# A fused convolution and maxout kernel: a reordered opening, a gate made a transfer, sums in three parts, one logarithm one group later, and a last copy split over two engines

## The chip, the cores and the metric

The kernel runs on one core of a Trainium2 chip. The metric is the device time of one execution in microseconds (us). Five engines work in order, each on its own list of instructions: PE (TensorE, matrix products), DVE (VectorE), ACT (ScalarE), POOL (GpSimd) and SP (SyncE, which here only issues transfers). An instruction waits on semaphores for what it needs, and everything behind it on its engine waits with it.

## What is computed

A dynamic convolution over the sequence is followed by a feed-forward layer with a maximum in it. Cut to what matters:

```
w = softmax(weight_gen, over the 7 taps)          # [8, 4160, 8 heads, 7]
y[s] = sum over k of w[s, k] * x[s - 6 + k]       # per head, 24 features each, D = 192
g = maximum(y @ w1, y @ w2)                       # 33280 tokens, 1024 hidden features
out = g @ w_out                                   # [33280, 192], float32
```

## The kernel before

**The tokens.** 33280 tokens lie as 128 partitions by 260 columns. Columns go in 17 batches of 16 (the last has 8), batches in units of 8 columns (of 4 in the first two batches and at the end). A tile of the hidden layer is 1024 values by 128 partitions; there are 260 tiles, in 90 groups, the first eight of two tiles and the others of three (the last of one).

**The softmax** is done as exp(w - ln(sum(exp(w)))): ACT takes the exponential (`exp_sum`, line 153), DVE the sums over taps (`red`, line 168), ACT the logarithm (`ln`, line 172), DVE the subtraction (`shift`, line 177) and ACT the final exponential into `en_t` (`weights`, line 191).

**The convolution.** DVE multiplies x by the weights for all 7 taps into `m_t` (`mul`, line 211). In the first two batches PE adds the taps, one unit at a time, while it transposes (`sum_transpose`, line 281), and ACT copies the result out of the accumulator (`sums_out`, line 293). From batch 2 on DVE adds the taps in three instructions (`adds`, lines 227, 233 and 236), a DMA transposes `y_t` into `yt` (line 245), and the work for later batches is put between the three additions by the `beside` callback: sums in two halves, subtractions in three parts.

**The feed-forward.** max(a, b) is written as a + relu(b - a). PE makes the hidden tiles (`hid_tile`, line 336) from `yt` and `wd` = w2 - w1, ACT applies relu (line 346), PE adds the product with w1 @ w_out (line 388) and the hidden part (line 376), ACT copies the result to `o_t` (line 434) and SP stores it. Half of the hidden part (`out_second`) starts only behind a `relay`, an empty instruction on ACT that waits for the other half.

**The gate.** After each transposing DMA, line 253 has POOL copy one column of `yt` into a small tile `gate`. POOL works in order, so the loads of x and of the weights behind it (lines 125 and 118) are issued only once the transposed unit is there.

**The opening.** Until the steady loop begins (group 8), the order of all work is a list of steps written out by hand, `OPENING`. A step is put on the list of its engine in that order. `lg lw lt xf` are loads issued by SP, `lx lo lh` loads issued by POOL (`@step` holds a load until that step is done). On ACT: `X` exponential, `l` logarithm, `W` weights, `c` casts of w1, `e` copy of a summed unit, `T` copies of turned weights, `r` relu, `V` copies of w1 transposed, `C` copies of w1 @ w_out, `xa` a cast of x, `B` the relay, `E` the copy of the results. On DVE: `n` sums, `s` subtraction, `m` products, `d` the difference w2 - w1, `xv` a cast of x. On PE: `k` products that only keep the clock up, `y` tap sums, `t` turned weights, `h` hidden tiles, `v` and `p` the w1 products, `A` and `D` the two halves of the result. So `W.0.12` is the weights of batch 0 from column 12, `r.3` is the relu of tile 3, and `m.0.0.1` is the second half of the products of the first unit.

The accumulators of `y` (all but the first half unit), `t.0`, `t.1`, `v`, `p` and `A` take turns in two buffers (tag `op`): each waits until the one two before it has been read out. `t.2` shares the buffer of `t.0`. The buffers of `h` take turns in two others.

**The loop** places the ACT softmax steps by a table `SOFTMAX_AT`, keyed by group and place: place 0 is ahead of the last relu of a group, place 1 after its result copy.

Of the kernel before, what the change touches and what calls it, by code (L numbers as in the profile page):

```python
# [9 lines left out]
FP32 = mybir.dt.float32  # L10
BF16 = mybir.dt.bfloat16
# [12 lines left out]
def kernel(  # L24
# [9 lines left out]
    nc = tc.nc  # L34
# [182 lines left out]
    def adds(b, o, first=False, beside=lambda i, of: None):  # L217


        w = dict(pieces(b))[o]  # L220
        n = w * D

        def taps(at, step, cnt):
            return _sub(m_t, K * o * D + at * n, [[step * n, cnt], [1, w * D]])

        beside(0, 3)
        nc.vector.tensor_tensor(out=taps(0, 1, 3), in0=taps(0, 1, 3), in1=taps(3, 1, 3), op=ALU.add)  # L227
        if first:
            return
        beside(1, 3)  # L230
        if b not in y_ts:
            y_ts[b] = py.tile([P, 16 * D], BF16, name="y_t", tag="y")
        nc.vector.tensor_tensor(out=taps(0, 2, 2), in0=taps(0, 2, 2), in1=taps(1, 5, 2), op=ALU.add)  # L233
        beside(2, 3)

        nc.vector.tensor_tensor(  # L236
            out=_sub(y_ts[b], o * D, [[64, 2], [P, 3 * w // 2], [1, 64]]),
            in0=taps(0, 1, 1), in1=taps(2, 1, 1), op=ALU.add,
        )

    def transpose(u):

        b, o, n = UNITS[u]
        yt = pyt.tile([P, 8 // 2 * 3 * P], BF16, name="yt", tag="yt")
        nc.sync.dma_start_transpose(
            out=yt[:, 0:n // 2 * 3 * P].rearrange("p (b t) -> p b t", t=P),
            in_=y_ts[b][:, o * D:(o + n) * D],
        )
        yt_ts[u] = yt
        while held:  # L250
            held.pop(0)()

        nc.gpsimd.tensor_copy(out=gate, in_=yt[:, 0:1])  # L253
# [11 lines left out]
        return slice(64 * j, 64 * j + 64)  # L265


    LEFT = (0, 1, 2, K - 1)

    def sum_transpose(u, i=None):  # L270

        b, o, n = UNITS[u]
        assert n == 4
        to = "h" if i == 0 else "o"
        yps = yps_of[u, i] = ps[to].tile([P, 1024], FP32, name="yps", tag="hd" if i == 0 else "op")
        ks = range(6) if i is None else range(3 * i, 3 * i + 3)
        for k in ks:
            for t in range(K):
                at = K * o * D + (t * 6 + k if i is None else (K * i + t) * 3 + k % 3) * P
                for r in range(2):  # L280
                    nc.tensor.matmul(  # L281
                        yps[:, r * 512 + k * 64:r * 512 + (k + 1) * 64],
                        lhsT=m_t[half(r), at:at + P], rhs=ident[half(r), half(r)],
                        start=(k == ks[0] and t == 0), stop=(t == K - 1),
                        skip_group_check=True,
                    )
# [129 lines left out]
    def evac(p, n):  # L416

        tile_, at = op_at[p]
        o = o_t[0]
        if p == NT // 2 - 1:  # L420

            nc.scalar.copy(out=_sub(o_last, 0, [[D, 2], [1, D]]),
                           in_=_sub(tile_, at, [[512, 2], [1, D]]))
            for j, eng in enumerate((nc.scalar, nc.sync)):
                eng.dma_start(
                    out=bass.AP(tensor=out.tensor, offset=dcol(place(p)[0] + 2 * j) * D, ap=[[CPP * D, P], [1, D]]),
                    in_=o_last[:, j * D:(j + 1) * D],
                )
            return
        runs = [[q for q in range(p, p + n) if column(2 * q)[0] == u]  # L430
                for u in range(column(2 * p)[0], column(2 * (p + n - 1))[0] + 1)]
        for qs in runs:
            c, h = place(qs[0])
            copied = nc.scalar.copy(out=_sub(o, c % 24 * D, [[D, len(qs)], [h * D, 2], [1, D]]),  # L434
                           in_=_sub(tile_, at + (qs[0] - p) * D, [[D, len(qs)], [512, 2], [1, D]]))
        stores = []
        for q in range(p, p + n):
            u, i, _ = column(2 * q)
            if u == NU - 2 and UNITS[u][2] == 8 and i % 2:
                stores.append((nc.sync, place(q)[0] - 1, [4 * D, 2], [1, 2 * D]))  # L440
            elif u < NU - 1 and i == UNITS[u][2] // 2 - 1:
                w = i + 1
                for k in range(0, 2 * w, w if u in PARTED else 2 * w):
                    stores.append((nc.sync, place(q)[0] - i + k, [1, (w if u in PARTED else 2 * w) * D]))
            if u == NU - 1:
                stores.append((nc.sync, place(q)[0], [2 * D, 2], [1, D]))
        for eng, c, *ap in stores:

            def issue(eng=eng, c=c, ap=ap, o=o):
                eng.dma_start(  # L450
                    out=bass.AP(tensor=out.tensor, offset=dcol(c) * D, ap=[[CPP * D, P], *ap]),
                    in_=_sub(o, c % 24 * D, ap),
                )

            if 3 <= u < NU - 3:
                held.append(issue)
            else:
                while u > 3 and held:
                    held.pop(0)()
                issue()  # L460
        return copied
# [80 lines left out]
    around = consts.tile([P, 2 * P], BF16, name="around")  # L542
    ident, swap = around[:, 0:P], around[:, 64:64 + P]
    zeros = consts.tile([P, PAD * D], BF16, name="zeros")
    gate = consts.tile([P, 1], FP32, name="gate")
    o_last = consts.tile([P, 2 * D], FP32, name="o_last")

    pstage = ctx.enter_context(ExitStack())
    stage = pstage.enter_context(tc.tile_pool(name="pstage", bufs=1))
# [13 lines left out]
    def load_w(h, wi):  # L563

        wsrc = (moe_w1, moe_w2)[wi]
        return nc.sync.dma_start(
            out=ws["E", wi][:, h * HF:(h + 1) * HF],
            in_=bass.AP(tensor=wsrc.tensor, offset=h * HF, ap=[[F, P], [1, HF]]),
        )

    def load_last(h, wi):

        wsrc = (moe_w1, moe_w2)[wi]
        return nc.sync.dma_start(  # L574
            out=ws["T", wi][half(h), :],
            in_=bass.AP(tensor=wsrc.tensor, offset=P * F + h * HF, ap=[[F, 64], [1, HF]]),
        )
# [124 lines left out]
    def results_buffer(_):  # L702
# [16 lines left out]
    }  # L719

    OPENING = """
        lg.0 xf.-6.6 xf.0.4 lt.1.0 lt.0.0 k.2 lw.0.1 k.19 lw.0.0 lt.1.1 lw.1.0 lt.0.1 X.0.0.2 k.1 n.0.0.2
        X.0.1.2 lw.1.1 k.1 k.2 n.0.1.2 l.0.0.2 s.0.0.2 xa.-6.4 l.0.1.2 W.0.0.0 lx.0.4.4@l.0.0.2 lg.1 xv.-2.6
        W.0.0.1 s.0.1.2 W.0.12 c.0 lx.0.12.4@W.0.12 W.0.8 m.0.0.0 m.0.0.1 W.0.4 y.0.0 y.0.1 c.2 e.0.0 c.1
        e.0.1 d.0 d.2 t.0 k.3 t.2 T.3 d.1 T.4 h.0 h.1 t.1 X.1 r.0 lx.0.8.4 T.1 lo.0 r.1 m.0.4 n.1 v.0 h.2
        lx.1.0.8 V.1 y.1 r.2 l.1 h.3 e.1 m.0.8 lg.2@l.1 s.1 V.0 m.0.12 r.3 h.4 W.1.0 m.1.0 y.2 h.5 r.4 p.0
        e.2 r.5 h.6 lx.1.8.8@r.4 lg.3@e.2 y.3 W.1.8 h.7 lh.2 C.1 C.0 C.2 A.3 W.1.4 X.2 r.6 e.3 B.3 m.1.4 h.8
        D.3 y.4 r.7 r.8 Z.0 E.3 n.2 X.3 l.2 m.1.8 A.4 e.4 W.1.12 lx.2.0.8.0@r.7 B.4 h.9 D.4 h.10 r.9 E.4 s.2
        r.10 lg.4@r.9 y.5 W.2.0 A.5 h.11 B.5 h.12 e.5 D.5 n.3 r.11 r.12 A.6 m.1.12 E.5 h.13 B.6 D.6 y.6 r.13
        E.6 h.14 e.6 l.3 lx.2.8.8@r.13 h.15 r.14 A.7 W.2.8 B.7 y.7 D.7 r.15 e.7 E.7  # L730
    """

    make_identity(nc, ident_f)
# [3 lines left out]
    for step in OPENING.split():  # L737
# [24 lines left out]
    def extra(t):  # L762

        u, k = TILES[t]
        b, o, n = UNITS[u]
        s = o + k

        if s == 0 and b + 1 < NB:
            mul(b + 1, 0)
        later = 0 if b < 4 else 5  # L770
        if s == later and b + 1 < NB:

            c = b + 1
            adds(c, 0, beside=lambda i, of: shift(c + 1, i, of) if c + 1 < NB else None)
        if s == 8 and b + 2 < NB:
            mul(b + 1, 8)
        if s == 8 + later and b + 2 < NB:
            adds(b + 1, 8, beside=lambda i, of: red(b + 3, i, 2) if b + 3 < NB and i < 2 else None)
        if s == 8 and b + 2 == NB:
            mul(b + 1, 4)  # L780
            adds(b + 1, 4)
        if k == n // 4 - 1 and 7 < u + 1 < NU:
            transpose(u + 1)
# [41 lines left out]
```

## Time and profile before

| what | value |
|---|---|
| median of 3 runs | 405.51 us (405.4 to 405.52) |
| the profiled execution | 405.37 us, with a span of 403.6 us |
| PE busy | 394.8 us, 98% of the span |
| DVE busy | 369.1 us, 91%, done at 376.3 us |
| ACT busy | 360.9 us, 89% |
| POOL busy | 72.3 us, of which the 30 gate copies 39.9 us |
| granted TensorE clock | 1.00 throughout |

The span is from the first instruction's start to the last one's end; 1.8 us of the profiled execution's time lie outside it. An engine's busy share over the whole span hides that the opening, the loop and the tail have different limits: PE is idle or on clock-keeping products for much of the first 30 us, and without a gap from then until the last product.

### The profile page before, as it was taken

Reading aid. Unit: us, or ns where it says so; the run is one execution under the profiler, and the core shown is the slowest. Engines: PE = TensorE matmul, PEld = TensorE weight load, DVE = VectorE, ACT = ScalarE, POOL = GpSimd, SP = SyncE. Lnnn points to the kernel's source line nnn. Section 1 sums busy time; section 2 is a strip of 40 time slices with the busy share of each in tenths; the row PEclk is TensorE's granted clock in tenths of the full one; section 3 lists DMA queues with packets and bytes.
Section 4 is the critical chain, followed back from the end, with each engine's and each line's share of the span. In section 5 each row is a group of like instructions: output and inputs, shape, how many; then the busy total and the mean of one; then the engine's idle time right before and its main releaser. Section 6 shows DMA issues by size and latency. Waiting matters only on the chain.

```text
span 403.6 us, 16321 instructions
## 1 busy us (share of the span) xinstructions
PE 394.8 (98%) x7499; PEld 321.3 (80%) x7499; DVE 369.1 (91%) x211; ACT 360.9 (89%) x466; POOL 72.3 (18%) x96
## 2 busy tenths in 40 slices
PE   7799999999999999999999999999999999999996
PEld 3589999777778777778777778877777877787996
DVE  5999999999999999999999999999999999998200
ACT  5999899999999989999899999989999899888872
POOL 3111031211122210222220122122012121200000
PEclk9999999999999999999999999999999999999999
DMA  8956468767768646864766667777457847558304
GB/s 262 222 140 151 120 124 167 183 164 133 190 110 222 182 79 129 240 187 80 217 187 107 141 192 193 99 215 198 81 115 228 178 80 200 141 106 193 104 31 169
DMA packets 60883, 63.16 MB, mean 157 GB/s; under 512 B 47641, under 2 KB 48665, under 8 KB 60816
## 3 DMA queue, kind: packets, MB, share of 16 engines
q1 hardware_dynamic: 52816, 40.15, 36.4%
q0 software_dynamic: 7856, 21.89, 27.4%
q8 instruction: 58, 0.95, 1.0%
q10 hardware_dynamic: 144, 0.10, 0.1%
q14 instruction: 9, 0.07, 0.1%
HBM read 36.55 MB, written 25.56 MB: 154 GB/s over the span
## 4 chain that ended last, share of the span: by engine, by line
PE 92%; ACT 5%; DMA 1%; SPq 1%; issue 0%
PE op_ps L376 42%; PE hdc L336 13%; PE hdb L336 13%; PE hda L336 13%; PE op_ps L388 8%; ACT rd_t L346 2%; DMA ws0E<-in_moe_w_dram 1%; PE hdp L336 1%; PE yps L281 1%; ACT en_t L191 1%; ACT yt L293 1%; ACT e_t L153 0%; ACT w1t L644 0%; SPq L574 0%; ACT w L622 0%
## 5 line engine op out<-in xcount | busy, mean ns | idle before, releaser
L376 PE MATMUL op_ps<-wo,rd_t 64*128 64x192 bf16 x4160 | 210.6, 243 | 0.0
L376 PEld LDWEIGHTS <-rd_t 64*128 64x128 bf16 x4160 | 181.0, 94 | 14.7
L211 DVE TENSOR_TENSOR m_t<-xb,en_t 128x10752 bf16<-128x10752 bf16 (+2 forms) x39 | 187.8, 4821 | 1.5 <-ACT en_t L191 1.4
L336 PEld LDWEIGHTS <-wd 64*128 64x128 bf16 x1824 | 96.8, 94 | 40.4 <-issue 2.5
L346 ACT ACTIVATE rd_t<-hdc 128x1024 bf16<-128x1024 f32 x82 | 84.1, 1025 | 17.8 <-PE hdc L336 16.2
L253 POOL CAST gate<-yt 128x1 f32<-128x1 bf16 x30 | 39.9, 1332 | 271.3 <-DMA yt<-y_t 271.3
L346 ACT ACTIVATE rd_t<-hda 128x1024 bf16<-128x1024 f32 x81 | 83.4, 1030 | 0.2 <-ACT o_t L434 0.2
L346 ACT ACTIVATE rd_t<-hdb 128x1024 bf16<-128x1024 f32 x81 | 83.5, 1031 | 0.0
L227 DVE TENSOR_TENSOR m_t<-m_t 128x4608 bf16<-128x4608 bf16 (+1 forms) x30 | 73.0, 2433 | 0.1
L336 PE MATMUL hdc<-yt,wd 64*128 64x512 bf16 (+1 forms) x552 | 67.9, 353 | 0.0
L434 ACT COPY o_t<-op_ps 128x384 f32<-128x384 f32 (+1 forms) x99 | 56.1, 577 | 12.4 <-PE op_ps L376 12.3
L336 PE MATMUL hdb<-yt,wd 64*128 64x512 bf16 (+1 forms) x540 | 67.1, 355 | 0.0
L336 PE MATMUL hda<-yt,wd 64*128 64x512 bf16 (+1 forms) x540 | 67.1, 355 | 0.0
L388 PE MATMUL op_ps<-w,yt 64*128 64x192 bf16 x780 | 55.5, 243 | 0.0
L388 PEld LDWEIGHTS <-yt 64*128 64x128 bf16 x780 | 39.0, 94 | 14.5 <-issue 0.3
L233 DVE TENSOR_TENSOR m_t<-m_t 128x3072 bf16<-128x3072 bf16 (+1 forms) x30 | 50.2, 1674 | 0.1
L191 ACT ACTIVATE en_t<-wg_t 128x896 bf16<-128x896 f32 (+3 forms) x48 | 35.7, 773 | 3.0 <-PE op_ps L376 2.0
L236 DVE TENSOR_TENSOR y_t<-m_t 128x1536 bf16<-128x1536 bf16 (+1 forms) x30 | 27.5, 916 | 0.6
L177 DVE TENSOR_TENSOR wg_t<-wg_t,sum_t 128x280 f32<-128x280 f32 (+6 forms) x46 | 22.2, 483 | 0.0
L168 DVE TENSOR_REDUCE sum_t<-e_t 128x64 f32<-128x448 f32 (+3 forms) x31 | 19.7, 639 | 2.3 <-ACT e_t L153 2.3
L125 POOL DMA_DIRECT2D xb<-in_x_dram x34 | 18.2, 537 | 17.3 <-ACT rd_t L346 11.0
L153 ACT ACTIVATE e_t<-wg_t 128x896 f32<-128x896 f32 (+2 forms) x18 | 15.9, 886 | 2.1 <-DMA wg_t<-in_weight_gen_dram 2.1
(40 smaller groups left out, 110.0 us busy)
## 6 DMA issues: line engine op xcount, KB each, us to landing
out_dram<-o_t SPq DMA_DIRECT2D x21, 768.0 KB, 4.3
xb<-in_x_dram POOLq DMA_DIRECT2D x30, 384.0 KB, 5.0
out_dram<-o_t SPq DMA_DIRECT2D x22, 384.0 KB, 3.7
wg_t<-in_weight_gen_dram POOLq DMA_DIRECT2D x13, 448.0 KB, 5.7
xb<-xb POOLq DMA_DIRECT2D x7, 288.0 KB, 5.1
wg_t<-in_weight_gen_dram SPq DMA_DIRECT2D x2, 448.0 KB, 5.2
xb<-in_x_dram POOLq DMA_DIRECT2D x4, 192.0 KB, 6.4
xs<-in_x_dram SPq DMA_DIRECT2D x1, 576.0 KB, 4.3
```

Of the source, the lines that this page charges most:

```text
L177: nc.vector.tensor_tensor(out=w_t, in0=w_t, in1=_sub(s_ts[b], hs.start, [[1, hs.stop - hs.start], [0, K]]), op=ALU.subtract)
L191: act = nc.scalar.activation(out=_sub(en_ts[b], (o * WGC + ((i or 0) * J + j) * N * K) * 2, [[2 * N, K], [2, N], [1, 2]]), in_=_sub(wg_ts[ ...
L211: return nc.vector.tensor_tensor(out=m_out, in0=x_in, in1=_sub(en_ts[b], at * H * 2, [[2, K * n * H], [0, G // 2], [1, 2]]), op=ALU.mult,)
L227: nc.vector.tensor_tensor(out=taps(0, 1, 3), in0=taps(0, 1, 3), in1=taps(3, 1, 3), op=ALU.add)
L233: nc.vector.tensor_tensor(out=taps(0, 2, 2), in0=taps(0, 2, 2), in1=taps(1, 5, 2), op=ALU.add)
L236: nc.vector.tensor_tensor(out=_sub(y_ts[b], o * D, [[64, 2], [P, 3 * w // 2], [1, 64]]), in0=taps(0, 1, 1), in1=taps(2, 1, 1), op=ALU.add,)
L253: nc.gpsimd.tensor_copy(out=gate, in_=yt[:, 0:1])
L336: nc.tensor.matmul(hid_out(t, f, j), lhsT=wd_at(j, s, f // 4, f % 4 * P, P), rhs=_sub(yt_ts[u][half(j), :], (s + j) % 3 * P, [[3 * P, w // ...
L346: relu_of[t0] = nc.scalar.activation(out=rd[:, k * 1024:(k + n) * 1024], in_=hd[:, at:at + n * 1024], func=AF.Relu)
L376: return nc.tensor.matmul(op_out(c), lhsT=rd[rows, k * 1024 + at:k * 1024 + at + P], rhs=wo[rows, f * D:(f + 1) * D], start=False, stop=(r ...
L388: nc.tensor.matmul(op_out(c + j), lhsT=yt_ts[u][half(j), (3 * i + (s + j) % 3) * P:(3 * i + (s + j) % 3 + 1) * P], rhs=w10[half(j), s * D: ...
L434: copied = nc.scalar.copy(out=_sub(o, c % 24 * D, [[D, len(qs)], [h * D, 2], [1, D]]), in_=_sub(tile_, at + (qs[0] - p) * D, [[D, len(qs)] ...
```

## The change

Five edits. In `OPENING` the steps stand in another order, and several loads are held by other steps. The gate becomes a transfer of two values issued by POOL. The sums of the loop are taken in three parts, one ahead of each of the three additions. The logarithm of batch 5 moves from group 16 to group 17. The last result is copied in two halves, one by ACT and one by DVE, into two tiles.

```diff
-        nc.gpsimd.tensor_copy(out=gate, in_=yt[:, 0:1])
+        nc.gpsimd.dma_start(out=gate, in_=yt[0:1, 0:2])
...
-            nc.scalar.copy(out=_sub(o_last, 0, [[D, 2], [1, D]]),
-                           in_=_sub(tile_, at, [[512, 2], [1, D]]))
-            for j, eng in enumerate((nc.scalar, nc.sync)):
+            for j, (eng, copy) in enumerate(((nc.scalar, nc.scalar.copy), (nc.sync, nc.vector.tensor_copy))):
+                copy(out=o_last[j], in_=tile_[:, at + 512 * j:at + 512 * j + D])
...
-        lg.0 xf.-6.6 xf.0.4 lt.1.0 lt.0.0 k.2 lw.0.1 k.19 lw.0.0 lt.1.1 lw.1.0 lt.0.1 X.0.0.2 k.1 n.0.0.2
-        X.0.1.2 lw.1.1 k.1 k.2 n.0.1.2 l.0.0.2 s.0.0.2 xa.-6.4 l.0.1.2 W.0.0.0 lx.0.4.4@l.0.0.2 lg.1 xv.-2.6
-        W.0.0.1 s.0.1.2 W.0.12 c.0 lx.0.12.4@W.0.12 W.0.8 m.0.0.0 m.0.0.1 W.0.4 y.0.0 y.0.1 c.2 e.0.0 c.1
-        e.0.1 d.0 d.2 t.0 k.3 t.2 T.3 d.1 T.4 h.0 h.1 t.1 X.1 r.0 lx.0.8.4 T.1 lo.0 r.1 m.0.4 n.1 v.0 h.2
-        lx.1.0.8 V.1 y.1 r.2 l.1 h.3 e.1 m.0.8 lg.2@l.1 s.1 V.0 m.0.12 r.3 h.4 W.1.0 m.1.0 y.2 h.5 r.4 p.0
-        e.2 r.5 h.6 lx.1.8.8@r.4 lg.3@e.2 y.3 W.1.8 h.7 lh.2 C.1 C.0 C.2 A.3 W.1.4 X.2 r.6 e.3 B.3 m.1.4 h.8
-        D.3 y.4 r.7 r.8 Z.0 E.3 n.2 X.3 l.2 m.1.8 A.4 e.4 W.1.12 lx.2.0.8.0@r.7 B.4 h.9 D.4 h.10 r.9 E.4 s.2
-        r.10 lg.4@r.9 y.5 W.2.0 A.5 h.11 B.5 h.12 e.5 D.5 n.3 r.11 r.12 A.6 m.1.12 E.5 h.13 B.6 D.6 y.6 r.13
-        E.6 h.14 e.6 l.3 lx.2.8.8@r.13 h.15 r.14 A.7 W.2.8 B.7 y.7 D.7 r.15 e.7 E.7
+        lg.0 k.2 xf.-6.6 xf.0.4 lt.1.0 lt.0.0 lw.0.1 lw.0.0 lt.1.1 lw.1.0 lt.0.1 X.0.0.2 n.0.0.2 X.0.1.2
+        lw.1.1 n.0.1.2 l.0.0.2 k.19 s.0.0.2 l.0.1.2 xa.-6.4 W.0.0.0 xv.-2.6 lx.0.4.4@xa.-6.4 lg.1 s.0.1.2
+        W.0.0.1 k.1 lx.0.12.4@W.0.0.1 c.0 m.0.0.0 c.2 d.0 m.0.0.1 y.0.0 t.0 k.3 W.0.4 e.0.0 W.0.12 k.2 y.0.1
+        d.2 W.0.8 e.0.1 t.2 d.1 T.4 T.3 t.1 T.1 h.0 k.1 h.1 c.1 lx.0.8.4@e.0.0 lg.2@e.0.1 lo.0 r.0 X.1 h.2
+        r.1 m.0.4 v.0 n.1 V.0 lx.1.0.8@r.1 y.1 r.2 l.1 h.3 e.1 m.0.8 r.3 V.1 s.1 m.0.12 h.4 W.1.0 y.2 r.4
+        W.1.8 m.1.0 h.5 p.0 e.2 h.6 C.2 C.1 y.3 lx.1.8.8@C.2 r.5 lg.3@W.1.0 lh.2 h.7 C.0 A.3 X.2 r.6 W.1.4
+        n.2 h.8 l.2 B.3 e.3 D.3 r.7 y.4 Z.0 E.3 A.4 m.1.4 X.3 W.1.12 h.9 B.4 r.8 e.4 m.1.8 r.9 D.4 s.2 lg.4
+        h.10 E.4 n.3 lx.2.0.8.0@r.8 r.10 y.5 h.11 W.2.0 A.5 B.5 h.12 e.5 D.5 r.11 A.6 l.3 h.13 E.5 r.12 B.6
+        W.2.8 D.6 h.14 E.6 m.1.12 y.6 r.13 e.6 h.15 A.7 lx.2.8.8@W.2.8 r.14 B.7 y.7 D.7 r.15 e.7 E.7
...
-        (9, 1): "X.4 W.3.0", (12, 0): "W.3.8 l.4", (14, 1): "X.5", (16, 0): "W.4.0", (16, 1): "l.5",
+        (9, 1): "X.4 W.3.0", (12, 0): "W.3.8 l.4", (14, 1): "X.5", (16, 0): "W.4.0", (17, 1): "l.5",
...
-            adds(b + 1, 8, beside=lambda i, of: red(b + 3, i, 2) if b + 3 < NB and i < 2 else None)
+            adds(b + 1, 8, beside=lambda i, of: red(b + 3, i, 3) if b + 3 < NB else None)
```

The diff also lets `sum_transpose` leave out taps of units in a set `fewer`, lets `load_w` load a whole matrix and `load_last` use another queue. No step uses these: the set stays empty, so PE has the same instructions in number and kind.

More of the change, by code (lines that the diff above doesn't have):

```diff
@@ L228, in adds @@
         if first:
+            fewer.add((b, o))
             return
@@ L265, in half @@
         return slice(64 * j, 64 * j + 64)
-    LEFT = (0, 1, 2, K - 1)
+    fewer = set()
     def sum_transpose(u, i=None):
@@ L276, in sum_transpose @@
         ks = range(6) if i is None else range(3 * i, 3 * i + 3)
+        taps = (0, 1, 2, K - 1) if (b, o) in fewer else range(K)
         for k in ks:
-            for t in range(K):
+            for t in taps:
                 at = K * o * D + (t * 6 + k if i is None else (K * i + t) * 3 + k % 3) * P
@@ L420, in evac @@
         if p == NT // 2 - 1:
-            nc.scalar.copy(out=_sub(o_last, 0, [[D, 2], [1, D]]),
-                           in_=_sub(tile_, at, [[512, 2], [1, D]]))
-            for j, eng in enumerate((nc.scalar, nc.sync)):
+            for j, (eng, copy) in enumerate(((nc.scalar, nc.scalar.copy), (nc.sync, nc.vector.tensor_copy))):
+                copy(out=o_last[j], in_=tile_[:, at + 512 * j:at + 512 * j + D])
                 eng.dma_start(
                     out=bass.AP(tensor=out.tensor, offset=dcol(place(p)[0] + 2 * j) * D, ap=[[CPP * D, P], [1, D]]),
-                    in_=o_last[:, j * D:(j + 1) * D],
+                    in_=o_last[j],
                 )
@@ L544 @@
     zeros = consts.tile([P, PAD * D], BF16, name="zeros")
-    gate = consts.tile([P, 1], FP32, name="gate")
-    o_last = consts.tile([P, 2 * D], FP32, name="o_last")
+    gate = consts.tile([1, 2], BF16, name="gate")
+    o_last = [consts.tile([P, D], FP32, name=f"o_last{j}") for j in range(2)]
     pstage = ctx.enter_context(ExitStack())
@@ L565, in load_w, with load_last @@
         wsrc = (moe_w1, moe_w2)[wi]
+        at, w = (0, F) if h == 2 else (h * HF, HF)
         return nc.sync.dma_start(
-            out=ws["E", wi][:, h * HF:(h + 1) * HF],
-            in_=bass.AP(tensor=wsrc.tensor, offset=h * HF, ap=[[F, P], [1, HF]]),
+            out=ws["E", wi][:, at:at + w],
+            in_=bass.AP(tensor=wsrc.tensor, offset=at, ap=[[F, P], [1, w]]),
         )
-    def load_last(h, wi):
+    def load_last(h, wi, act=0):
         wsrc = (moe_w1, moe_w2)[wi]
-        return nc.sync.dma_start(
+        return (nc.scalar if act else nc.sync).dma_start(
             out=ws["T", wi][half(h), :],
```

## The prediction

> **What bounds the kernel now.** I read the page's busy digits first, then PE's waits.
>
> ```profile
> PE   7799999999999999999999999999999999999996
> DVE  5999999999999999999999999999999999998200
> PE hdp L336 <- ACT yt L293: 1.3, 2, 0.8
> PE hdp L336 <- ACT rd_t L346: 0.4, 1, 0.4
> ```
>
> PE loses time in the first quarters only. The windows of the trace give it 10.0 of 10.0 us busy from 30 to 40 us, and every later window up to 395 us full as well; its last wait is that of h.8 on r.6, ending at 29.36 us. So the end is set by when PE gets through the opening, as long as the other engines keep ahead. In the opening the one without gaps is ACT, by its own timeline from 8 to 31 us:
>
> ```profile
> 9.95 0.62 ACT L622 CAST w<-ws0E 128x512 bf16<-128x512 f32 x1 [1.02 <-DMA ws0E<-in_moe_w_dram]
> 10.48 1.29 ACT L191 ACTIVATE en_t<-wg_t 128x224 bf16<-128x224 f32 x4
> ...
> 13.45 1.08 ACT L614 CAST wd<-turned 128x512 bf16<-128x512 f32 x2
> 14.54 0.95 ACT L153 ACTIVATE e_t<-wg_t 128x896 f32<-128x896 f32 x1
> 15.40 1.01 ACT L346 ACTIVATE rd_t<-hdp 128x1024 bf16<-128x1024 f32 x1
> ...
> 19.51 0.82 ACT L293 CAST yt<-yps 128x768 bf16<-128x768 f32 x1
> 20.19 0.84 ACT L644 COPY w1t<-tp 128x768 bf16<-128x768 bf16 x1
> 20.88 1.08 ACT L346 ACTIVATE rd_t<-hdp 128x1024 bf16<-128x1024 f32 x1
> ```
>
> The first cast, c.0, waits for w1 until 9.93 us; from there ACT is never idle until 41 us. Each line starts about 0.1 us before the one above it ends, so steps are counted by start-to-start distance: relu 0.91 (20.88 to 21.79), `e` 0.68 (19.51 to 20.19), a pair of weights 0.60 (10.48 to 11.67 for two), `c` 0.52, `T` 0.47, the half `e` 0.38, `X` 0.86, `V` 0.68, `l` 0.20.
>
> DVE is close behind PE. Unit 30 is the tightest: its transposed tile is seen by the gate at 316.04 us and its first hidden tile starts at 317.49.
>
> ```profile
> 316.04 0.96 POOL L253 CAST gate<-yt 128x1 f32<-128x1 bf16 x1 [9.85 <-DMA yt<-y_t]
> 317.49 0.83 PE L336 MATMUL hda<-yt,wd 64*128 64x512 bf16 x6
> ```
>
> From unit 8, used 13.5 us after it landed, the lead falls to 1.5 us here, about 0.55 us a unit. A DVE that falls 1.5 us further behind PE becomes the bound.
>
> **The opening: +2.0 us.** I walked both lists with these distances; for the old order the walk stays within 0.5 us of the trace.
>
> The new list puts c.0 and c.2 ahead of W.0.4, W.0.12 and W.0.8. The load c.0 needs cannot land earlier: until 9.93 us only SP's loads move (the first POOL packet is at 10.1 us) and their order is unchanged. W.0.12, done at 8.23 in the old order while ACT waited, now falls behind the wait, and ACT idles from 7.7 to 9.95. Then c.0 9.95, c.2 10.48, W.0.4 10.98, e.0.0 11.58, W.0.12 11.96, W.0.8 12.56, e.0.1 13.16, T.4 13.54, T.3 14.01, done at 14.62.
>
> Now a new wait. t.1 takes the accumulator of t.0, so PE may run it only when T.3 has read that out: 14.66, 0.39 us. T.1 is next on ACT and waits for t.1: it starts at 15.09 where ACT was free at 14.48, 0.6 us lost. On PE h.0, the keep-warm product and h.1 stand behind t.1. Then c.1, r.0 (16.1, was 15.40), X.1 (17.0, was 14.54), r.1, V.0, r.2, l.1, e.1, r.3 and V.1, which starts at 22.1 and ends at 22.97. The old list had both `V` done at 21.03. The difference of 1.94 is W.0.12 (0.60), r.3 now ahead of the second `V` (0.91) and the wait (0.6), less some 0.15 of rounding.
>
> y.2 on PE uses the accumulator that both `V` read, and started at 21.03. At 22.97 it takes with it, without a gap, h.5, p.0, h.6, y.3, h.7 and A.3: +1.94. Here the new order gives something back: W.1.4 stands behind r.6, so h.8 follows A.3 at once, and the old order's gap ahead of h.8 (0.5 us) is gone: +1.4. But W.1.4 (0.60) has only moved behind r.6, ahead of r.7 and r.11, and A.6 needs r.11. ACT's count from r.6 to r.11 was 10.3 us and becomes 10.9; r.11 then ends after 41.1 and by the walk at 41.7, so A.6 starts at 41.1 to 41.8 where it was 39.56: +1.6 to +2.2. I take +2.0. Afterwards PE has no gap to win it back in.
>
> DVE: X.1 is late, and n.1 stands ahead of m.0.8; DVE, free at 16.6, waits to 18.0 (+1.4). n.2 then waits for X.2 and m.1.4 for W.1.4, 0.6 us each: m.2.0 comes 2.6 us late. That is 0.6 us more than PE, and leaves unit 30 about 0.9 of its 1.5 us.
>
> d.0 ahead of m.0.0.1 puts y.0.1 at 12.1 for 11.2, under ACT's e.0.1 at 13.16: nothing. The held x loads: lx.0.4.4 goes out at 7.0 instead of 5.94 (landed at 12.88) for m.0.4 at 13.8; even at 14.5 it ends ahead of n.1's wait. lx.0.8.4 goes out near 12.1 and lx.1.0.8 near 19; with the 5.0 to 6.4 us from issue to landing of POOL's x loads they are there by 18.5 and 25.4; m.0.8 needs one at 19, m.1.0 the other at 25.7. w_out, near 15, has 10 us to p.0. lx.2.0.8, held by r.8 at 36, lands at about 41 for m.2.0 at 41.6: the one with little cover, 0.5 us if it takes the 5.7 of the weights' loads. On POOL everything behind it has 10 us. Low end +1.0 (no wait for t.1, no lag at r.11), high end +2.6 (c.0's load 0.4 later as POOL's packets come between, and 0.2 at m.2.0).
>
> **Sums in three parts: nothing on PE, but an ACT wait of +0.3.** DVE's rows:
>
> ```profile
> L168 DVE TENSOR_REDUCE sum_t<-e_t 128x64 f32<-128x448 f32 x24 | 14.7, 616 | 2.3 <-ACT e_t L153 2.3
> L168 DVE TENSOR_REDUCE sum_t<-e_t 128x32 f32<-128x224 f32 x2 | 0.8, 383 | 0.0
> 201.53 0.61 DVE L168 TENSOR_REDUCE sum_t<-e_t 128x64 f32<-128x448 f32 x1
> 202.06 1.75 DVE L233 TENSOR_TENSOR m_t<-m_t 128x3072 bf16<-128x3072 bf16 x1
> 203.84 0.96 DVE L236 TENSOR_TENSOR y_t<-m_t 128x1536 bf16<-128x1536 bf16 x1
> ```
>
> From 448 and 224 elements a sum costs 0.15 us plus 1.04 ns an element, so 280 elements 0.44 and 336 elements 0.50. Independent neighbours overlap by 0.085, so two halves occupy 1.06 us and three parts 0.36 + 0.36 + 0.42 = 1.14. But the last addition, which needs the one before it, starts 0.03 after its end (202.06 + 1.75 to 203.84) instead of 0.085 ahead; a third part between them fills that 0.12. Net -0.04 us a batch; over the 11 batches to unit 30 DVE gains 0.45. The other end: each added sum costs its whole 0.15 and fills nothing, 1.7 us. I take the first, as the neighbours overlap in all rows.
>
> The Trainium skill speaks against it ("VectorE: DVE Perf Modes", "The DRAIN you can't avoid" and its errata section): the next operation starts only when the pipe is empty, a fixed term of about 150 cycles is paid for each, so minimise their count. The intercept agrees; the overlapping starts do not. By the rule 11 more cost about 1.7 us (an estimate).
>
> What does change is the end of a batch's last sum: later by the middle addition and the third part less the shorter parts before, 1.75 us. Logarithms on ACT wait for it:
>
> ```profile
> 203.25 0.31 ACT L172 ACTIVATE sum_t<-sum_t 128x128 f32<-128x128 f32 x1
> 206.32 0.47 ACT L434 COPY o_t<-op_ps 128x384 f32<-128x384 f32 x1
> ```
>
> That is l.10, 1.1 us after its last sum (201.53 + 0.61). l.5 had 0.8 us and moves a group later: it starts near 88 instead of 84.6, ahead of its subtraction at 92.06, behind 4 us more PE work: nothing. l.10 stays: 1.1 - 1.75 + 0.25 (six batches of 0.04) - 0.6 (DVE's lag) is -1.0, an ACT wait of 1.0. Behind it stand relus a, b, c and the copy of 206.32, done at 206.80; PE writes that accumulator again at 207.14. So 0.34 is hidden and up to 0.6 us reaches PE. l.15 has 0.65 by the same reckoning and some 0.8 of slack behind it. Between 0 (DVE as late as PE) and 0.6 I take +0.3, the lag being itself a difference of two walks.
>
> **The gate: 0.** A cast takes 1.33 us as it ends with DVE's product (197.02 + 1.64 against 192.87 + 5.75); a POOL issue takes 0.54 us. The loads leave about 0.8 us earlier, and the loop shows no wait for them. If the transfer delayed them by the 5 us of a load, they would still be 6 us ahead of the next transpose; between -0.1 and +0.1.
>
> The Trainium skill ("SBUF — State Buffer", "Who interferes with whom") says that a tensor_tensor with two SBUF inputs and a GpSimd read exclude each other, whoever starts first. That could repay DVE up to 30 times; here the products take 5.754 us with a gate beside them or without, so I count none.
>
> **The tail: -0.15.** The copy at 400.05 of 384 values takes 0.48; half of it on ACT, from 0.31 (64x192), on DVE unknown between 0.2 and 0.5 (its 1152-value cast takes 0.76): -0.25 to 0.
>
> **Sum.** 405.37 for the profiled execution + 2.0 + 0.3 + 0 - 0.15 = 407.5; the median of the runs lies 0.14 above that execution, so 407.65, given as 407.6.
>
> **Rivals.**
> 1. The opening costs half (+1.0): T.1's wait or r.11's lag is covered. For it: the old order had 0.5 us of gap to give. 406.5.
> 2. DVE becomes the bound: each added sum costs its 0.15 in full. Unit 30's 1.5 us less 0.6 of lag less 1.7 is -0.8, so PE waits 0.8 us: 405.5 + 2.0 + 0.8 + 0.3 - 0.15 = 408.4. It decides once DVE loses over 0.9 us on PE. Against it: the overlapping starts. The skill's rule on operation count names this way.
> 3. Faster: the weights land earlier because x and w_out are held back, and ACT starts c.0 right behind W.0.0.1. With w1 at 7.7 instead of 9.93 the lag at y.2 is 1.94 - 2.2 = -0.3; with the gap ahead of h.8 gone that is -0.8, and -0.15 at the tail: 404.6. It decides from a landing of about 8.6 on. Against it: nothing but SP's loads moved before 9.93.
> 4. ACT's lag is made up by its 11% of idle time: 405.5. Against it: PE has no gap after 30 us.
>
> **Chances.** Forecast 0.58, rival 1 0.18, rival 2 0.13, rival 3 0.06, rival 4 0.05. A measurement tells 0.2% (0.8 us) from no change: slower takes the first three (0.89) less 0.01 for the edge of rival 1, same that and rival 4 (0.06), faster rival 3 (0.06). The range 406.2 to 408.7 holds the first three with their bounds.
>
> **What would show it.** c.0 at 9.95 with 2 us of ACT idle ahead; T.1 waiting for t.1; n.1 waiting for X.1 by over 1 us; the last `V` ending near 23 us; PE without gaps from about 43 us; l.10 waiting for DVE; gate issues of 0.5 us. It is wrong if w1 lands before 9 us, or if unit 30 starts on its landing.

## The result, and the profile after

| | median | range, executions | ratio to before | 95% interval |
|---|---|---|---|---|
| before | 405.51 us | 405.21 to 407.94, 12 | | |
| after | 410.24 us | 406.68 to 412.85, 12 | 1.009 | 1.0069 to 1.0112 |

By the medians the change costs 4.7 us (1.2%). The ratio of 1.009 compares the means of the executions in the chip's usual, fast state; one of after's twelve (412.85 us) was in a slower one. The profiled execution took 409.98 us with a span of 408.2 us (before 405.37 and 403.6). Slower was forecast, but by 2.1 us, and the range ended at 408.7.

I read the page first: the busy digits of PE and DVE of the changed kernel, in the 40 slices, and its row of the queue that brings the engines' own instructions (packets, MB, share of 16 engines' span).

```profile
PE   7898799999999999999999999999999999999996
DVE  5899989999999999999999999999999999988300
q8 instruction: 58, 0.95, 0.9%
```

The second 8 of PE's row stands at 31 to 41 us and the 7 behind it at 41 to 51 us, where before had nines. The opening's order was expected to cost PE most of its time ahead of 31 us (+1.4 of the +2.0). Next the waits of PE in the same kernel (waited for: us in total, times, the longest):

```profile
PE yps L283 <- issue: 2.6, 3, 1.3
PE op_ps L378 <- issue: 0.9, 1, 0.9
```

Before has no such line. "Issue" means that nothing which the profile shows was waited for: no semaphore, no other engine. PE's own timeline of after has the four places:

```profile
31.50 0.53 PE L283 MATMUL yps<-around,m_t 64*128 64x64 bf16 x24
32.37 1.05 PE L283 MATMUL yps<-around,m_t 64*128 64x64 bf16 x60 [0.33 <-issue]
...
36.53 0.26 PE L283 MATMUL yps<-around,m_t 64*128 64x64 bf16 x6
37.74 1.31 PE L283 MATMUL yps<-around,m_t 64*128 64x64 bf16 x78 [0.94 <-issue]
...
41.09 0.34 PE L378 MATMUL op_ps<-wo,rd_t 64*128 64x192 bf16 x4
42.29 0.67 PE L378 MATMUL op_ps<-wo,rd_t 64*128 64x192 bf16 x12 [0.85 <-issue]
...
48.45 1.11 PE L283 MATMUL yps<-around,m_t 64*128 64x64 bf16 x64
50.84 0.47 PE L283 MATMUL yps<-around,m_t 64*128 64x64 bf16 x20 [1.28 <-issue]
```

The same four steps, y.4, y.5, D.5 and y.7, run whole in PE's timeline of before:

```profile
31.33 1.41 PE L281 MATMUL yps<-around,m_t 64*128 64x64 bf16 x84
...
35.46 1.40 PE L281 MATMUL yps<-around,m_t 64*128 64x64 bf16 x84
...
38.90 0.84 PE L376 MATMUL op_ps<-wo,rd_t 64*128 64x192 bf16 x16
...
45.23 1.40 PE L281 MATMUL yps<-around,m_t 64*128 64x64 bf16 x84
```

After the change PE stops in the middle of a step, with the step's operands there: y.4 after 24 of its 84 products, y.5 after 6, D.5 after 4 of 16, y.7 after 64. Counted from the start of the list the stops come behind 607, 735, 863 and 1119 matmuls: 128, 128 and 256 apart. Each matmul has its own weight load, so 128 of them are 256 instructions; the queue brought 58 packets of 16 KB for the 15,000 instructions of PE, some 256 a packet. PE stops where one packet ends.

The time adds up by PE's lag behind before, step by step. At h.8 the lag was 0.17 us. y.4 put 0.51 on it, y.5 1.11, D.5 1.03 and y.7 1.46, together 4.11. The 0.17 of h.8 and waits for other engines between the stops make the remaining 0.57. From y.7 to the last product the lag is 4.68 throughout, and the tail behind PE is 0.07 shorter: 405.37 + 4.68 - 0.07 = 409.98, the profiled execution's time.

Why the packets were late is read from the trace's records of that queue. In the table "passed" is when PE went past the place 256 instructions ahead of the one named (the request, as I infer it), then come start and end of the packet, and when PE went on at the place named.

| at matmul | before: passed | packet | PE there | after: passed | packet | PE there |
|---|---|---|---|---|---|---|
| 607 (y.4) | 26.25 | 28.55 to 29.48 | 31.67 | 26.80 | 30.11 to 31.01 | 32.37, stopped |
| 735 (y.5) | 31.67 | 32.23 to 33.51 | 35.54 | 32.37 | 34.83 to 36.24 | 37.74, stopped |
| 863 (D.5) | 35.54 | 36.38 to 37.31 | 39.01 | 37.74 | 39.95 to 40.90 | 42.29, stopped |
| 991 (y.6) | 39.01 | 39.71 to 40.74 | 42.74 | 42.29 | 43.42 to 44.52 | 46.44 |
| 1119 (y.7) | 42.74 | 43.41 to 44.45 | 46.15 | 46.44 | 48.67 to 49.64 | 50.84, stopped |

PE goes on 1.2 to 1.5 us after the packet's end at the earliest. In before a packet starts 0.55 to 0.84 us after its request, but for the first row (2.29). In after it takes 2.2 to 3.3 us in all four stopped rows. What was in the way are POOL's loads. This is POOL's timeline of after, with the issue of each:

```profile
25.93 0.53 POOL L125 DMA_DIRECT2D xb<-in_x_dram  x1 [6.81 <-ACT w L669]
26.45 0.55 POOL L118 DMA_DIRECT2D wg_t<-in_weight_gen_dram  x1
31.34 0.54 POOL L139 DMA_DIRECT2D xb<-xb  x1 [4.34 <-DMA xb<-in_x_dram]
31.88 0.54 POOL L118 DMA_DIRECT2D wg_t<-in_weight_gen_dram  x1
36.08 0.53 POOL L125 DMA_DIRECT2D xb<-in_x_dram  x1 [3.67 <-ACT rd_t L348]
45.61 0.53 POOL L125 DMA_DIRECT2D xb<-in_x_dram  x1 [9.00 <-ACT en_t L191]
```

They are lx.1.8.8, lg.3, the halo (a copy of the last six columns of x, line 139), lg.4, lx.2.0.8 and lx.2.8.8. In before the same six left at these times, with lx.2.0.8 ahead of lg.4:

```profile
23.77 0.53 POOL L125 DMA_DIRECT2D xb<-in_x_dram  x1 [3.28 <-ACT rd_t L346]
24.45 0.54 POOL L118 DMA_DIRECT2D wg_t<-in_weight_gen_dram  x1 [0.16 <-issue]
28.99 0.54 POOL L139 DMA_DIRECT2D xb<-xb  x1 [4.00 <-DMA xb<-in_x_dram]
31.22 0.53 POOL L125 DMA_DIRECT2D xb<-in_x_dram  x1 [1.68 <-ACT rd_t L346]
36.08 0.54 POOL L118 DMA_DIRECT2D wg_t<-in_weight_gen_dram  x1 [4.32 <-ACT rd_t L346]
42.66 0.53 POOL L125 DMA_DIRECT2D xb<-in_x_dram  x1 [6.05 <-ACT rd_t L346]
```

A load's packets begin about 1.2 us behind its issue. In before the packets of POOL's loads move in stretches with breaks between (25.00 to 29.61 us, 30.11 to 31.01, 32.46 to 35.93, 37.33 to 39.42, 43.90 to 46.69), and all but the first of the fetches above start in a break. In after the stretches have grown together: 528 packets without a break from 27.16 to 40.62, then 46.86 to 50.51. The four late fetches start inside these. From 32.4 to 34.8 us, between the second request and its packet, the DMA view of after has no packet of the instruction queue, and POOL's loads have nearly all of the 16 engines:

```profile
q0 software_dynamic: 101, 0.44, 91.1%
```

In before, lg.4 left at 36.08 us, when the request of 35.54 had been made, while in after it leaves at 31.88, and its packets, from 33.49 to 37.70, fill the time between those of the halo (to 33.41) and of lx.2.0.8 (from 37.32).

### The profile page after: what moved, and what is told of

It reads as the page before. It is cut to its first block, busy times and chain, and to the rows that moved or that the text cites. A ratio compares the mean times of both kernels' runs of the same rounds, so it can differ in the third digit from the quotient of the medians.

```text
span 408.2 us, 16344 instructions
## 1 busy us (share of the span) xinstructions
PE 397.0 (97%) x7499; PEld 321.9 (79%) x7499; DVE 369.3 (90%) x225; ACT 361.1 (88%) x466; POOL 49.2 (12%) x96
## 4 chain that ended last, share of the span: by engine, by line
PE 92%; ACT 4%; DMA 2%; issue 1%; DVE 0%; POOL 0%; POOLq 0%
PE op_ps L378 41%; PE hdc L338 13%; PE hda L338 13%; PE hdb L338 13%; PE op_ps L390 8%; PE warm L676 2%; DMA wg_t<-in_weight_gen_dram 2%; ACT rd_t L348 1%; PE yps L283 1%; PE hdp L338 1%; ACT e_t L153 0%; ACT yt L295 0%; ACT w1t L646 0%; ACT en_t L191 0%; DVE around L738 0%
## 5 line engine op out<-in xcount | busy, mean ns | idle before, releaser
L254 POOL DMA_DIRECT2D gate<-yt x30 | 15.3, 511 | 295.7 <-DMA yt<-y_t 295.7
L168 DVE TENSOR_REDUCE sum_t<-e_t 128x40 f32<-128x280 f32 (+6 forms) x44 | 21.6, 493 | 4.8 <-ACT e_t L153 4.8
```

The lines of the kernel that those rows point to most:

```text
L168: nc.vector.reduce_sum(out=s_ts[b][:, hs], in_=_sub(e_ts[b], at, ap), axis=AX.X)
```

## The experiments

Theory F, formed from this trace: the loss lies in the loads that the new list holds differently (lx.1.8.8, lg.3, lx.2.0.8, lg.4, lx.2.8.8), as they stand in front of PE's own instructions; the order of the work itself costs little. The rivals are the order of the work, as predicted, and the other three parts of the change.

### Halves of the change: e1 and e2

e1 is the changed kernel with before's `OPENING`. e2 is before with the new `OPENING`, so without the gate, the thirds, l.5 and the tail.

> The changed kernel with the opening's list of the kernel before; gate as a transfer, sums in three parts, logarithm of batch 5 later and the split last copy stay. Theory F (the time is lost where PE waits for its own instructions, because instruction fetches of 16 KB queue behind bulk loads that the new opening issues at other moments): no such stall in the first 60 us, and the whole kernel within 0.5 us of the kernel before, about 405.4 (tail -0.15, and up to +0.3 if the logarithm of batch 10 now waits for the third part of its sum). Rival G (the gate as a transfer or the three parts bring the loss): 407 us or more, with the lost time after 60 us.

> The kernel before with only the new opening's list. Theory F: the same stalls within PE's steps as in the changed kernel (some 4 us in its profile, between 30 and 55 us), 408 to 411 us. Rival G: close to 405.5 us.

Measured: e1 405.48 us, ratio 1.000 (0.9987 to 1.0013). Its profiled execution took 1476 us and isn't read, so that e1 has no stops in it is inferred from its time. e2 410.69 us, ratio 1.0095 (1.0057 to 1.0132), with PE stopped at the same four matmuls, 607, 735, 863 and 1119. The whole loss is in the opening's list; the other four edits together cost nothing that can be measured.

### The order without the holds: e3

```diff
-        ... lx.1.8.8@C.2 r.5 lg.3@W.1.0 lh.2 ... W.1.12 h.9 ... s.2 lg.4
-        h.10 E.4 n.3 lx.2.0.8.0@r.8 r.10 y.5 ... A.7 lx.2.8.8@W.2.8 r.14
+        ... lx.1.8.8@r.4 r.5 lg.3@e.2 lh.2 ... W.1.12 lx.2.0.8.0@r.7 h.9 ... s.2
+        h.10 E.4 n.3 r.10 lg.4@r.9 y.5 ... A.7 lx.2.8.8@r.13 r.14
```

> The changed kernel; of the opening only the holds and places of five loads go back to those before (x of batch 1 from column 8 behind r.4, weights of batch 3 behind e.2, x of batch 2 from 0 behind r.7, weights of batch 4 behind r.9, x of batch 2 from 8 behind r.13). The order of all work on PE, ACT and DVE stays the new one. Theory F: fetches again wait 0.5 to 1 us for their turn (2.3 at most), no stall over 0.3 us within a step of PE; what is left is the new order's own delay of 0.6 us less the tail: 406 us, at most 406.5. Rival O (the new order of work itself brings the loss): 409 to 410.5 us, as the changed kernel.

Measured: 406.47 us, ratio 1.0021 (1.0013 to 1.003), in executions from 406.02 to 407.25. PE doesn't stop for "issue" at all; its timeline of e3 has the steps whole:

```profile
31.07 1.41 PE L283 MATMUL yps<-around,m_t 64*128 64x64 bf16 x84
...
35.59 1.40 PE L283 MATMUL yps<-around,m_t 64*128 64x64 bf16 x84
```

So five holds carry 3.8 of the 4.7 us. The order of the work leaves PE 0.59 us behind after D.7, and l.10 adds 0.13: 405.37 + 0.72 - 0.07 = 406.02, that execution's time. Some 0.2 of the 0.59 still belong to late packets: at matmuls 863 and 1119 PE goes on 1.30 and 1.41 us after the packet's end, each time 0.11 us later than its pace in before.

### Two loads sooner in before: e4

```diff
-        r.10 lg.4@r.9 y.5 ... lx.2.8.8@r.13
+        r.10 lg.4@E.3 y.5 ... lx.2.8.8@E.5
```

> The kernel before with two loads issued earlier: weights of batch 4 behind E.3 (32.5 us instead of 36.1) and x of batch 2 from column 8 behind E.5 (40.9 instead of 42.7), so that their packets are under way when fetches 5 and 7 are asked for (35.5 and 42.7 us). Nothing else is changed and nothing waits for these loads. Theory F: these two fetches wait 1.5 to 2.5 us instead of 0.7 to 0.8, and with 0.4 us to spare PE stalls for 0.8 to 1.5 us at each: 406.5 to 408 us. Rival O: no stall, 405.5 us.

Measured: 407.94 us, ratio 1.0059 (1.0038 to 1.0079); the profiled execution took 406.88. Its stops are at matmuls 863 (0.3 us) and 1119:

```profile
47.69 0.47 PE L281 MATMUL yps<-around,m_t 64*128 64x64 bf16 x20 [1.24 <-issue]
```

Two holds put into the old list bring two of the stops, with no step of the work moved. So loads alone make the stops come and, in e3, go.

### Does the stop belong to the list or to the step: e5

```diff
-        l.0.0.2 k.19 s.0.0.2
+        l.0.0.2 k.16 q.48 s.0.0.2
```

`q` is a step that the kernel has but doesn't use: small products that only keep PE busy. They stand in PE's idle time.

> The changed kernel with 45 more matmuls on PE in its idle time at the start (three of the 19 keep-warm products make way for 48 small ones of 64 columns); nothing else moves. Theory F (PE stands still because the next packet of its own instructions is late): the stalls belong to places in PE's list and not to steps, so they stay at matmuls 607, 735, 863 and 1119 of the list and fall 45 matmuls earlier in the work: in h.8 after 7 of its 12, in h.9 after 1, in h.11 after 5, in y.7 after 19 of 84 (where a fetch is late again; the sizes may change, as the requests move by 0.7 us against the loads). Rival S (something that these steps need, a product or an accumulator, is late): the stalls stay in y.4 after 24 of 84, y.5 after 6, D.5 after 4 of 16 and y.7 after 64 of 84. Time by either 408.5 to 411.5 us.

Measured: 408.6 us, one execution. One stop of "issue" is left, at matmul 863 of the longer list as foretold, which is now in h.11 after 5 of 12. PE's timeline of e5:

```profile
37.44 0.49 PE L338 MATMUL hdp<-yt,wd 64*128 64x256 bf16 x5
39.43 0.59 PE L338 MATMUL hdp<-yt,wd 64*128 64x256 bf16 x7 [1.50 <-issue]
```

The steps that stopped without the added products, y.4, y.5, D.5 and y.7, run whole here. The place follows the count and not the step; rival S falls. That the other three stops went was not foretold: the first request came at 26.38 us and its packet at 27.15, ahead of the loads' packets (from 27.38). With that stop gone the next request came 1.5 us sooner, and its packet fell into a break.

### One load alone: e6

```diff
-        A.7 lx.2.8.8@W.2.8 r.14
+        A.7 lx.2.8.8@r.13 r.14
```

> The changed kernel with one load put back: lx.2.8.8 is held by r.13 again, in place of W.2.8, and so leaves about 2 us later. Theory F: each stall has its own load. The stall in y.7 (1.4 us) goes or falls under 0.5 us, those in y.4, y.5 and D.5 (2.6 us together) stay within 0.4 us each; 408.8 us, 408.2 to 409.4. Rival (the stalls come from the sum of all loads, or from something else): y.7 still stalls by over 1 us, 409.8 to 410.6.

Measured: 408.62 us, ratio 1.0065 (1.005 to 1.0079). The three earlier stops stayed (0.58, 0.97 and 0.85 us of idle time), and y.7's fell from 1.28 to 0.19:

```profile
38.02 1.31 PE L283 MATMUL yps<-around,m_t 64*128 64x64 bf16 x78 [0.97 <-issue]
42.57 0.67 PE L378 MATMUL op_ps<-wo,rd_t 64*128 64x192 bf16 x12 [0.85 <-issue]
50.03 0.47 PE L283 MATMUL yps<-around,m_t 64*128 64x64 bf16 x20 [0.19 <-issue]
```

So this stop goes with this one load. For the other three no run moves one load alone; e4 moves two loads and has two stops. In e6 the load left 0.5 us behind the request in place of 0.8 ahead of it, and the packet took 0.68 us to start in place of 2.23.

### The logarithm's place: e7

Before's opening with the other parts, and l.5 at (16, 1) again. The first run's profiled execution took 696 us and isn't read; the second run, e7b, is there for its profile.

> Before's opening with the other three parts of the change, but the logarithm of batch 5 in its old place. Both theories: its sum in three parts ends 1.7 us later, so ACT waits for it, by 0.5 to 1.7 us (in before it had 0.8 us to spare). Theory W (the wait reaches PE): 0.3 to 0.8 us more than 405.5, a gap on PE near 85 to 90 us. Theory H (hidden, as PE has the accumulators to go on): 405.3 to 405.7, no gap on PE.

> The kernel with l.5 in its old place again, for its profile. By the interval measured (0.9995 to 1.0013) the wait is hidden: ACT waits 0.5 to 1.7 us for the last part of batch 5's sum and PE has no gap of over 0.2 us between 80 and 95 us. If PE has one of 0.3 us or more there, the wait reaches it.

Measured: e7 406.16 us, ratio 1.0004 (0.9995 to 1.0013); e7b, one execution, 406.76 us. Its w1 load landed late (c.0 ran at 10.93 us for 9.95), and PE carries 0.98 us from there. At 90 us the lag goes from 0.98 to 1.47. ACT and PE there, in the timeline of e7b:

```profile
86.48 0.31 ACT L172 ACTIVATE sum_t<-sum_t 128x128 f32<-128x128 f32 x1 [0.76 <-DVE sum_t L168]
...
89.95 0.42 PE L390 MATMUL op_ps<-w,yt 64*128 64x192 bf16 x6 [0.30 <-ACT o_t L435]
```

So the wait is not hidden: theory W by the trace, 0.49 us on PE, though the timing alone (0.12% would be 0.0012, inside its interval) can't tell it from nothing. By this one trace, l.5 in its old place would cost 0.49 us.

### One quarter of the weights moved: e8, e9, e10, e11

The prediction counted 0.5 us for W.1.4 going behind r.6. e8 does that alone, in before's list with the other parts:

```diff
-        A.3 W.1.4 X.2 r.6 e.3
+        A.3 X.2 r.6 W.1.4 e.3
```

> Before's opening with the other three parts of the change and one step moved in it: the quarter W.1.4 stands behind r.6 as in the new list. Theory G (my prediction's step: what the gap ahead of h.8 gives back is lost again at A.6, as ACT does the same work up to r.11): the gap of 0.3 to 0.5 us ahead of h.8 is gone, and a wait of 0.2 to 0.5 us for a relu or e stands between y.4 and A.6; 405.3 to 405.6. Theory K (kept): PE is 0.4 us ahead from h.8 to the end, 405.0 to 405.2. For the other parts: gate transfers of 0.5 us, l.10 and l.15 with waits of at most 0.5 us on ACT and no gap on PE, 3.49 us from PE's end to the span's end where before had 3.56.

Measured: 407.17 us, ratio 1.0035 (1.0011 to 1.0058). Both theories missed: the step costs 1.4 us. The profiled execution was the slowest (410.61 us; the other nine 406.89 to 407.86) and has four stops of "issue", at the same places as after. In that execution w1 landed late (c.0 ran at 10.54 us) and PE was 0.59 us behind before until h.7, so the first request came 0.59 us later. The closed gap brought PE back to before's time at matmul 607 (31.70 us for 31.67), and the packet, which ended at 30.57 for 29.48, wasn't ready. e9 takes the two loads out of the way:

```diff
-        r.3 h.4 ... h.6 lx.1.8.8@r.4 lg.3@e.2 y.3 W.1.8 h.7 lh.2 C.1 C.0
+        r.3 lx.1.8.8@r.3 h.4 ... h.6 y.3 W.1.8 h.7 C.1 lg.3@C.1 lh.2 C.0
```

> The kernel with the one quarter moved, and two loads moved with it: lx.1.8.8 is held by r.3 instead of r.4 and leaves 1.5 us sooner, lg.3 is held by C.1 instead of e.2 and leaves 1.5 us later, so that neither lies in front of the fetch that PE asks for near 26.3 us. Theory F: that fetch then starts within 1.2 us of its request (2.3 in before, 2.8 with the quarter moved alone), y.4 doesn't stall at matmul 607, PE keeps the 0.3 to 0.5 us won ahead of h.8 unless a later fetch is late, and the time falls from 407.2 to 405.0 to 405.7. Rival (the moved quarter costs by itself, by the product m.1.4 that comes 2.5 us later on DVE): 406.9 to 407.4 with the loads moved too.

Measured: 407.31 us, ratio 1.0032 (1.0017 to 1.0047); the profiled execution took 406.92. Half of it came as foretold: the fetch started 0.64 us after its request and no stop is left. But the time stayed, and the trace gives two other reasons, on PE and ACT:

```profile
32.48 0.42 PE L390 MATMUL op_ps<-w,yt 64*128 64x192 bf16 x6 [0.42 <-ACT o_t L435]
```
```profile
205.30 0.31 ACT L172 ACTIVATE sum_t<-sum_t 128x128 f32<-128x128 f32 x1 [2.06 <-DVE sum_t L168]
```

At A.4 PE waits for an accumulator that ACT reads out no sooner, so the 0.57 us won ahead of h.8 is gone: 0.11 us ahead of before up to A.3, 0.68 at h.8, 0.11 again at A.4 (theory G of e8). And with n.2 behind the later m.1.4, DVE runs 1.79 us late; l.10 waits for its three-part sum, and PE's lag goes from -0.11 to 1.62 there. The rival named the product m.1.4, and it was right. e10 moves l.10 a group later in e9, and e11 does so in e8:

```diff
-        (44, 1): "l.10", (45, 1): "W.9.8",
+        (45, 1): "W.9.8 l.10",
```

> The kernel with the quarter and two loads moved, and l.10 one group later. Theory L (what is left of the loss there is the wait for l.10: with n.2 behind m.1.4 DVE is 1.8 us late, and the three-part sum ends after ACT gets to its logarithm, by 2.1 us, 1.7 us of it on PE): the wait goes and the time falls from 407.3 to 405.2 to 405.8. Rival (DVE's lag costs PE elsewhere, at unit 30 or at l.15, or the 1.7 us was of that one execution): 406.6 to 407.4.

> The kernel with the quarter moved alone, and l.10 one group later. Theory L (its usual executions, at 407.2, lose to the wait for l.10 like the one above, and only its slowest, which was the one profiled, to late fetches): 405.2 to 405.9. Theory F (its usual executions lose to late fetches, 1.4 us on average): 406.6 to 407.4 with l.10 moved too.

Measured: e10 406.72 us, 1.0032 (1.002 to 1.0044); e11 406.66 us, 1.0027 (1.0008 to 1.0045). Against before neither gained on e9 and e8. In the traces l.10 waits for nothing, and the next tight logarithm waits in its place: l.15, in e10 and then in e11:

```profile
323.30 0.28 ACT L172 ACTIVATE sum_t<-sum_t 128x96 f32<-128x96 f32 x1 [2.31 <-DVE sum_t L168]
```
```profile
323.42 0.28 ACT L172 ACTIVATE sum_t<-sum_t 128x96 f32<-128x96 f32 x1 [2.83 <-DVE sum_t L168]
```

PE's lag grows there by 0.78 and 1.32 us. e10's trace also has one stop, at matmul 1119 (0.34 us of idle time, 0.52 on the lag): its lag of 1.43 at the end is 0.13 up to there, 0.52 and 0.78 (405.37 + 1.43 - 0.07 = 406.73, that execution's time but for 0.01). e11 has e8's loads and no stop. So a late DVE is enough for the usual loss of e8, and late packets come on top in some executions; for those of e8 that weren't profiled this is argued from e9 and e11, not shown. No version beat before: e1 equals it, and it is the best that has the change's other parts.

## Why the prediction was wrong

**The opening, +2.0: the direction was right, the cause wrong.** That it came out slower as forecast is mostly owed to a cause that the prediction didn't have. By steps:

- c.0 waiting for w1, with W.0.12 fallen behind it: right. ACT's timeline of after:

```profile
9.79 0.62 ACT L624 CAST w<-ws0E 128x512 bf16<-128x512 f32 x1 [1.94 <-DMA ws0E<-in_moe_w_dram]
```

- T.1 waiting for t.1, 0.6 us lost: wrong. t.1 was released by the copy of y.0.1 and not by T.3, and ran at 13.68 us, ahead of T.3 (the second of ACT's two casts here); T.1 started at 14.48, without a wait:

```profile
13.53 1.08 ACT L616 CAST wd<-turned 128x512 bf16<-128x512 f32 x2
13.68 0.38 PE L608 MATMUL turned<-wd,around 128*128 128x512 bf16 x1 [0.25 <-ACT yt L295]
14.48 0.62 ACT L618 CAST wd<-turned 128x512 bf16<-128x512 f32 x1
```

  So the section on the kernel before has it wrong for this list that each accumulator waits for the one two before it: t.1 took the buffer of y.0.1, the one right before it, which had been read out first.

- y.2 using the accumulator that both `V` read: wrong. The last `V` did run late (21.66 to 22.49 us; 22.1 to 22.97 was forecast), but y.2 started ahead of it, at 21.57: +0.54, not +1.94.

```profile
21.57 1.41 PE L283 MATMUL yps<-around,m_t 64*128 64x64 bf16 x84
21.66 0.82 ACT L646 COPY w1t<-tp 128x768 bf16<-128x768 bf16 x1
```

  I took the turn of the buffers from counting steps and never held it against a row; in before, y.2 and the end of `V` merely fell on the same 21.03.
- The gap ahead of h.8 gone: right (h.7 0.73 late, h.8 0.17 late). r.11's lag reaching A.6 as +1.6 to +2.2: wrong in size. Without the stops, in e3, A.6 is 0.23 late. DVE, 2.6 us late at m.2.0 by the forecast, was 2.0 late; its wait for X.1 was 0.2 us, not 1.4.

The order alone gives +0.6 by the trace and +0.2% by timing (e3): rival 1's size (406.47 us for its 406.5), less than the forecast; but T.1's wait was not covered, as rival 1 has it, it was absent. The step that failed outright is the one on the held loads: it put them at nothing, or 0.5 us at lx.2.0.8, and they cost 3.8 of the 4.7 us (e3). It asked of each load only whether its own reader would have it in time ("On POOL everything behind it has 10 us"), and for the readers that was nearly right: m.2.0 waited 0.64 us. It never asked what else the same DMA engines carry. The row that should have been read is on the page of before, under the DMA queues:

```profile
q8 instruction: 58, 0.95, 1.0%
```

One per cent of the DMA time looked like nothing. But it is a stream with a deadline: from 31 to 46 us before had 0.4 to 0.9 us of slack on each packet (PE's arrival less the packet's end and 1.3 us), and moving five loads took it: lg.4 left 4.2 us sooner, the other four 2.0 to 4.9 us later. The Trainium skill has the mechanism ("Runtime: NRT & Kernel Launch", "Instruction fetch mechanics"): instructions are refilled in blocks of 16 KiB, 256 instructions, over DMA while the engine runs. The block size agrees with the stops 128 matmuls apart. It also says that crossing a block is mostly hidden; here it cost 4.11 us in one execution, so the measurement decides.

**"Afterwards PE has no gap"** (from about 43 us): wrong for the same reason, the last stop ends at 50.84.

**Sums in three parts: right on DVE, cancelled on ACT.** A unit of DVE's work with sums takes 11.79 us (from the end of one `y_t` at 196.71 to the next at 208.50), 11.86 in before: -0.06 us a batch for the -0.04 forecast. Unit 30 had 3.38 us of lead for 1.57, but PE was 4.68 us late there; in e3, with PE 0.72 late, the lead is 1.71 (landed at 316.50, used at 318.21). Rival 2, a DVE that pays for each added sum in full, falls; in after too each sum overlaps its neighbour (the sum of 202.29 ends at 202.73, the addition behind it starts at 202.65). The ACT wait of 1.0 us for l.10, +0.3 on PE, did not come in after: PE's own stops made ACT later than DVE by more, and l.10 had 0.3 us to spare. It is real where PE is on time: 0.13 us on PE in e3 and 1.73 in e9. So the mechanism held and its size depends on how late DVE is against PE. l.5 at nothing: right, and 0.49 us if it hadn't moved (e7b).

**The gate: right, 0.** The group of the gate transfers in after (busy, mean ns, then the wait ahead) shows 0.51 us for the 1.33 before, and e1 is at 1.000 with it:

```profile
L254 POOL DMA_DIRECT2D gate<-yt x30 | 15.3, 511 | 295.7 <-DMA yt<-y_t 295.7
```

**The tail, -0.15: the size was off, -0.07, and not for the reason given.** The halves don't run side by side. DVE's waits for ACT's, in the timeline of after:

```profile
404.73 0.32 ACT L425 COPY o_last<-op_ps 128x192 f32<-128x192 f32 x1
```
```profile
405.08 0.36 DVE L425 COPY o_last<-op_ps 128x192 f32<-128x192 f32 x1 [24.14 <-ACT o_last L425]
```

The last store lands 2.57 us after PE's end, as in before; what is shorter is the stretch behind it.

**Rival 3** (weights earlier) fell as forecast: c.0 ran at 9.79. **Rival 4** (lag made up) is half true of the order: 0.6 of 2.0 us remained.

## What to carry to other kernels

PE's own instructions come over the DMA engines in 16 KB packets with a deadline. Where PE runs short instructions without a gap and a profile shows it stopping for "issue" in the middle of a step, count instructions between the stops and look at which loads were issued just ahead. When a load is moved, ask what else is due on the DMA engines then, not only when its reader needs it. And a step ahead of which a gap is closed may give nothing: in these runs the next accumulator, the next packet or the next logarithm took it back.

## What was not expected of the hardware

- A fetch of 16 KB takes 0.9 to 1.5 us. In these traces it started 0.3 to 1.3 us after the request that I infer where no load, or only the end of one, moved in between, and 2.1 to 3.3 us after it at each stop of over 0.35 us. The fetch for matmul 607 waited 2.3 us in before as well; PE came there 5.4 us after the request, and didn't stop. From 32.4 to 34.8 us the loads' 101 packets took 91.1% of 16 engines, 0.35 us each (2.4 x 16 x 0.911 / 101), so the fetch of that stretch waited as long as seven of them. The Trainium skill ("DMA: Bandwidth & Descriptors", "Queues, rings and completion order") says that an engine takes turns between its queues, a whole packet from each. The Trainium skill counts there 9 to 17 descriptors to such a packet, and a load of x here is 144 of the profile's packets (128 rows and 16 of 4 bytes), nine for each engine if they are shared evenly. If one of the profile's packets is what the Trainium skill calls a descriptor there, a whole packet would take about 2.8 us (an estimate, 8 x 0.35), the size of the waits. It isn't shown: for lg.4 and lx.2.8.8 one of the 16 small packets starts behind the fetch's end (37.83 us for 35.77 to 36.44 of the others; 50.49 for 49.21 to 49.73), so the fetch seems to have gone in ahead of the load's end there. What sets the wait stays open.
- Kernels with stops in their trace vary more between executions: after ran from 406.68 to 412.85 us and e8 from 406.89 to 410.61, e3, whose trace has no stop, from 406.02 to 407.25. That the stops make the difference isn't shown, as one execution of each has a trace. The margin is small. For matmul 735 the request in before came at 31.67 us and the packet at 32.22, 0.24 ahead of the loads' stretch at 32.46. In e8's profiled execution the request came at 32.17, the stretch began at 33.02, and the packet started at 35.44, inside it.
- The landing of w1 differs by more than a microsecond between these traces (c.0 at 9.54 in e3, 9.95 in before, 10.93 in e7b), and PE carries the difference to the end: 0.98 us in e7b.
